# Sinkhorn attention and token mixer: X of two batches turned by SyncE transfers, step order searched anew

## The chip, the cores and the metric

The kernel runs on one core of one Trainium2 chip. A time is the device time of one execution in microseconds; the time before is the median of three runs, 105.33 us (105.27 to 105.39).

## The reference

Four batches of eight heads, 768 positions, 64 features per head. A sort matrix P of 8 by 8 per head mixes blocks of 96 positions of k and v, attention stays within a block, and its result x goes through a linear token mixer and an output product.

```python
P = sort_net
for _ in range(5):
    P = np.exp(P - np.max(P, axis=-1, keepdims=True))
    P = P / (np.sum(P, axis=-1, keepdims=True) + 1e-09)
    P = P / (np.sum(P, axis=-2, keepdims=True) + 1e-09)
k_sorted = np.einsum('bhij,bhjcd->bhicd', P, k_b)      # v alike
scores = scale * np.matmul(q_b, k_sb.transpose(0, 1, 2, 4, 3))
attn = np.exp(scores - max) / (sum + 1e-09)             # within a block
x = np.matmul(attn, v_sb)                               # then [batch, 768, 512]
wq, wk = x @ w_q, x @ w_k
W_tok = scale * np.einsum('bsd,btd->bst', wq, wk)
mixed = np.einsum('bst,btd->bsd', W_tok, x)
out = np.maximum(mixed, 0.0) @ w_out
```

## The kernel before, in words

The whole program is a list of steps in the string ORDER, one batch at a time being one digit. A loop at the end takes each word, say `T21:7`, and calls the function of its letter (`u_T`) with batch 2, part 1 and PSUM bank 7. Batches are counted from 0, so batch 2 is the third. Capital letters are matmuls on TensorE. Small letters are mostly the copies out of PSUM, with the engine behind the colon (A ScalarE, D VectorE, G GpSimd, S SyncE). Every engine and every DMA queue takes its steps in the order of the list; between engines, semaphores hold a step until its inputs are there and its PSUM bank or tile has been read. So the list fixes both what runs beside what, and what stands behind a step that waits.

The steps of one batch, in the order in which they depend on each other:

- `lq`, `lk`, `lv` (u_l, L220): GpSimd issues the loads of q, k, v of a batch from HBM, cast to bf16, 768 KB each as written. `lp` and `lo` load the weights. Qn, Kn and Vn have three buffers each.
- `Q`/`q`: q turned to QT on TensorE, copied out. Four parts, one per pair of heads. `K`/`k`: k sorted and turned to KT. `n` forms M, the sort matrix spread over masks, on GpSimd for batches 1 to 3.
- `V`/`v`: v sorted to Vs in three parts (batches 1 to 3). `R` (u_R, L313): six SyncE transfers per batch (1 to 3) that bring Vs into VT's layout, SBUF to SBUF, 132 KB each. Batch 0 takes `Y`/`y` and `F`/`f` on TensorE instead.
- `S`/`e`: scores and their exp into E, seven parts. `P`: E times VT into PSUM, five parts, with a column of row sums. `r` (reciprocal) and `x` (scaling, into X) on VectorE.
- `T`/`t` (u_T, L390; u_t, L394): X turned to XT, one part per pair of heads: eight transposing matmuls of 96x96 into one bank, then a copy.
- `J`/`j`: q and k projections from XT into qkT, in two halves, each needing all four parts of XT, one per matmul. `d`: half of qkT shifted by 64 partitions to qD, by SyncE or VectorE. `W`/`w`, `G`/`g`: the token mixer's inner product A from X. `H`/`h`: A times qkT and qD, with the relu, into mixT in three parts.
- `O`/`o`: output product, six per batch, into `ot` (four slots of 512 KB). `s` (u_s, L466): SyncE stores.
- `Z` is filler on TensorE while it has nothing to do, and `a`, `c`, `A`, `B`, `u`, `i` are the Sinkhorn loop and set-up at the start.

X and XT have two buffers each, as have QT, KT, VT and E. A function `u_D` (L386) that turns X by a transposing DMA, for two pairs of heads at once, is there; the ORDER of before doesn't use it. SyncE carries, in order: the sort matrix, six `R` for each of batches 1 to 3, two `d` for each of batches 0 to 2, and among these the stores. The last functions, a check of the softmax sums and a general path behind it, are not touched.

Of the kernel before, what the change touches and what calls it, by code (L numbers as in the profile page):

```python
# [14 lines left out]
NMIX = 2  # L15
SPQ = False
SPLIT = 6

ORDER = """
i02:D lq0 i00:G c00:D a01:A c01:D A00:0 a02:A:0 c02:D a03:A Z09:0 Q00:0 c03:D Q01:1 a04:A c04:D lk0  # L20
a05:A Q03:7 Q02:6 q01:A:1 c05:D Z06:2 B00:1 n00:D:1 n01:D:1 Z02:2 K00:2 K01:4 q00:A:0 k00:A:2
n02:D:1 u00:D:1 i03:G n03:D:1 K03:0 K02:2 k01:A:4 k02:D:2 k03:A:0 S00:4 S02:0 e00:A:4 q02:D:6 lv0
e02:A:0 Y02:2 q03:D:7 Y01:4 lv1 Y00:6 y01:D:4 Y03:0 y02:A:2 S04:2 y00:A:6 lk1 lq1 n10:G n11:G y03:D:0 S03:4
F01:6 F00:7 e04:A:2 S01:0 F03:2 e03:A:4 e01:A:0 f01:D:6 f00:D:7 V11:3 V12:5 f03:D:2 F02:7 P00:0
v11:A:3 v12:D:5 S05:2 f02:A:7 e05:A:2 r00:D:0 V10:4 n21:G P01:6 K13:2 x00:D:0 r01:D:6 P02:0
x01:D:6 v10:A:4 r02:D:0 K10:4 K12:6 k13:A:2 P03:2 x02:D:0 r03:D:2 k10:A:4 K11:4 k12:D:6 T01:0
T00:1 lp Q11:6 k11:A:4 t00:A:1 S06:4 U00:7 R12:S Q12:1 R15:S e06:A:4 R11:S x03:D:2 P04:2 t01:D:0
Q13:0 Q10:4 q11:A:6 r04:D:2 z01:A:7 S12:5 q12:D:1 x04:D:2 q13:A:0 U01:7 q10:D:4 z02:D:7 T02:1 T03:0
e12:A:5 t02:D:1 t03:D:0 lq2 S11:2 S10:4 S13:6 Q22:1 Q21:0 e11:A:2 q21:D:0 Q23:2 e10:A:4 q22:D:1
J00:3 e13:A:6 R10:S R14:S n20:G R13:S S16:4 e16:A:4 S15:0 j00:D:3 P11:6 S14:3 J01:5 e15:A:0 q23:D:2  # L30
e14:A:3 P12:0 r11:D:6 lk2 K23:2 j01:A:5 x11:D:6 K21:6 r12:D:0 P13:4 k23:A:2 K20:2 x12:D:0 k21:A:6
r13:D:4 n30:G K22:0 Q20:6 x13:D:4 W00:7 k20:A:2 lv2 k22:A:0 P14:2 lq3 V20:4 V22:0 d00:S q20:D:6
r14:D:2 W01:7 x14:D:2 V21:2 T12:6 v22:D:0 t12:D:6 v20:A:4 P10:4 S25:0 v21:A:2 S26:2 T13:6 r10:D:4
w00:A:7 T11:7 x10:D:4 d01:S e26:A:2 S23:2 n31:G e25:A:0 Q30:4 G00:5 S21:0 t13:D:6 e23:A:2 t11:D:7
S24:6 lk3 e21:A:0 G01:5 Q31:3 lv3 e24:A:6 g00:D:5 Q33:2 q31:D:3 S22:0 T10:5 e22:A:0 S20:6 q33:D:2
t10:D:5 K32:2 R21:S K31:0 J11:5 k32:A:2 R20:S q30:D:4 R22:S H00:2 Q32:4 e20:A:6 k31:D:0 lo j11:D:5
h00:A:2 R23:S K30:0 R24:S H01:6 q32:D:4 K33:4 h01:A:6 R25:S k30:D:0 P21:2 J10:0 V31:6 k33:A:4 P23:4
j10:A:0 v31:A:6 r21:D:2 P22:0 d10:S x21:D:2 r23:D:4 V32:2 W10:6 v32:A:2 W11:6 O01:7 x23:D:4 w10:A:6
V30:4 r22:D:0 v30:A:4 x22:D:0 o01:D:7 O02:2 S34:0 o02:D:2 H02:6 e34:A:0 h02:D:6 S32:3 O03:5 e32:A:3
o03:A:5 P20:0 T21:7 P24:2 r20:D:0 T22:4 t21:A:7 G10:5 G11:5 x20:D:0 r24:D:2 d11:S g10:D:5 S36:6  # L40
R32:S t22:A:4 S30:0 e36:A:6 R35:S O00:4 x24:D:2 S31:5 e30:A:0 R30:S H11:2 H10:0 O05:7 o00:D:4 T20:4
h11:D:2 o05:D:7 e31:A:5 R34:S T23:5 h10:A:0 t20:A:4 t23:A:5 S35:2 e35:A:2 R31:S S33:0 H12:6 e33:A:0
s01:S O04:4 J20:5 O10:3 s00:S j20:A:5 R33:S P31:0 J21:5 o10:A:3 P32:2 h12:D:6 O15:6 r31:D:0 o04:D:4
j21:A:5 r32:D:2 o15:A:6 x31:D:0 P33:4 r33:D:4 O12:7 o12:A:7 P30:0 x33:D:4 s02:S O13:6 d20:S P34:4
W20:7 x32:D:2 W21:7 r34:D:4 d21:S o13:A:6 T31:2 w20:D:7 O14:3 t31:D:2 r30:D:0 O11:7 G20:2 x30:D:0
G21:2 o11:A:7 s10:S x34:D:4 T30:7 o14:A:3 g20:A:2 t30:A:7 T32:0 T33:1 t32:D:0 t33:D:1 H21:4 H20:2
H22:6 h20:D:2 s11:S J30:0 J31:1 h22:D:6 O20:2 j30:D:0 O21:3 h21:A:4 W30:0 O22:7 j31:A:1 d31:D
w30:A:0 W31:0 o22:D:7 w31:D:0 O24:1 o20:A:2 o21:A:3 o24:A:1 G30:7 G31:7 g30:D:7 O23:0 d30:D H30:4
h30:A:4 o23:D:0 H31:2 s12:S h31:D:2 O25:7 s20:S H32:0 s21:S O31:4 o25:A:7 h32:D:0 O30:7 o31:D:4
s22:S s31:S O34:1 o34:A:1 o30:D:7 O32:4 O35:0 o32:A:4 s30:S o35:A:0 s34:S s32:S s35:S O33:4 o33:A:4  # L50
s33:S
"""


# [1 line left out]
def kernel(  # L56
# [12 lines left out]
    B, H, S, D = q.shape  # L69
    NB = sort_net.shape[-1]  # L70
    BLK = S // NB
# [29 lines left out]
    def tiles(name, n, shape, dtype=BF16):  # L101
        return [sb.tile(shape, dtype, name=f"{name}{i}") for i in range(n)]

    PS = psp.tile([P, 8, 512], FP32, name="ps")
    ENG = {"A": nc.scalar, "D": nc.vector, "G": nc.gpsimd, "S": nc.sync}
# [13 lines left out]
    X = tiles("X", 2, [BLK, NP, NB, P])  # L119
    XT = tiles("XT", 2, [P, PT, S])  # L120
# [7 lines left out]
    if SPQ:  # L128

        q32 = XT[0].rearrange("p t s -> p (t s)").bitcast(FP32).rearrange("p (h r d) -> p h r d", r=R6, d=D)  # L130
        nc.sync.dma_start(out=q32.rearrange("p h r d -> p h (r d)"),
                          in_=q[0, 0:H // 2].rearrange("h (p r) d -> p h (r d)", p=P))
# [251 lines left out]


    def u_D(b, n, e, bank):  # L386
        ENG[e].dma_start(out=XT[b % 2][:, 2 * n:2 * n + 2, :].rearrange("p k (i c) -> p (k i) c", c=BLK),
                         in_=X[b % 2][:, 2 * n:2 * n + 2].rearrange("c k i m -> c (k i m)"), transpose=True)

    def u_T(b, n, bank):  # L390
        for i in range(NB):
# [56 lines left out]
    def osplit(b, n):  # L448

        r, m = n % 10, n // 10  # L450
        return (r, slice(m * DM // 2, (m + 1) * DM // 2)) if b == B - 1 and r >= SPLIT else (r, slice(0, DM))

# [6 lines left out]
    def oslot(b, n):  # L459
        return ot[(b * 3 + n // 2) % NOT]  # L460
# [4 lines left out]

    def u_s(b, n, e, bank):  # L466
        od = out[b].rearrange("(p r) e -> p r e", r=R6)
        if b < B - 1:
            ENG[e].dma_start(out=od[:, 2 * n:2 * n + 2, :], in_=oslot(b, 2 * n))
        else:  # L470
            r, c = osplit(b, n)
            ENG[e].dma_start(out=od[:, r, c], in_=oslot(b, r)[:, r % 2, c])
# [172 lines left out]
    for item in ORDER.split():  # L645
# [5 lines left out]
        b, n = int(name[1]), int(name[2:])  # L651
# [41 lines left out]
```

## Time and profile before

| what | value |
|---|---|
| median of three runs | 105.33 us |
| the profiled execution: its time, its span | 105.29 us, 103.5 us |
| TensorE matmuls | 86.7 us, 84% of the span |
| VectorE | 71.8 us, 69% |
| ScalarE | 69.2 us, 67% |
| GpSimd | 25.4 us, 25% |
| chain of waits: TensorE, DMA, GpSimd | 44%, 39%, 6% |
| HBM read, written | 20.19 MB, 6.29 MB |
| granted TensorE clock | 0.998 |

The busy shares of three engines lie close together and are means over two different stages, so they don't say what bounds; the slices and the chain of waits do. [...] A DMA's row on SyncE is the time in which SyncE issues it, and its landing is told apart from that. Times in a timeline or chain are from the start of the span.

### The profile page before, as it was taken

The page shows a single profiled execution, that of the slowest core. Times are in us where ns is not written, and L with a number is a line of the kernel's source. Part 1 is how long each engine was busy: PE and PEld are TensorE (multiplying, and loading weights), DVE is VectorE, ACT ScalarE, POOL GpSimd, SP SyncE. Part 2 cuts the span into 40 slices and gives each one's busy share as a digit, 9 for nine tenths or more (in the row PEclk, how much of TensorE's full clock was granted, in tenths as well). Part 3 has the DMA queues.
Part 4 walks back from the last instruction along what each step waited for, and adds up shares of the span by engine and source line. Part 5 has one row for each costly group of instructions (what it writes and reads, how often), then busy time and mean ns, then how long its engine had stood idle before and what let it go on. Part 6 is the DMA issues. An engine that isn't in the chain of part 4 may idle for free.

```text
span 103.5 us, 3508 instructions
## 1 busy us (share of the span) xinstructions
PE 86.7 (84%) x1485; PEld 60.3 (58%) x1493; DVE 71.8 (69%) x142; ACT 69.2 (67%) x98; POOL 25.4 (25%) x42
## 2 busy tenths in 40 slices
PE   0297977996959699999969899999999999999930
PEld 0135366895838577898745675856667575543410
DVE  2676667889956578989559498777389979368400
ACT  4222479998668868979849688989944282633440
POOL 5992054991199500000000000000000272000000
PEclk9999999999999999999999999999999999999999
DMA  0899999999999999999999933737042077047782
GB/s 3 88 199 204 204 204 205 203 206 203 237 232 244 206 202 204 209 210 206 241 247 228 208 77 100 224 142 255 6 176 65 6 301 307 24 185 301 299 321 99
DMA packets 18593, 19.35 MB, mean 187 GB/s; under 512 B 912, under 2 KB 16656, under 8 KB 18576
## 3 DMA queue, kind: packets, MB, share of 16 engines
q0 software_dynamic: 13296, 10.09, 63.6%
q1 hardware_dynamic: 5280, 9.03, 25.2%
q8 instruction: 11, 0.18, 0.7%
q14 instruction: 6, 0.05, 0.1%
HBM read 20.19 MB, written 6.29 MB: 256 GB/s over the span
## 4 chain that ended last, share of the span: by engine, by line
PE 44%; DMA 39%; POOL 6%; ACT 3%; SPq 2%; issue 2%; POOLq 0%; ACTq 0%
PE ps L156 44%; DMA Kn<-in_k_dram 18%; DMA Vn<-in_v_dram 14%; DMA VT<-Vs 7%; SPq L314 2%; POOL Vn L231 2%; POOL M L252 1%; POOL Qn L231 1%; ACT Vs L160 1%; POOL Kn L231 1%; ACT KT L160 1%; ACT ot L160 1%; POOL E L211 1%; ACT wk L160 0%; POOL VT L217 0%
## 5 line engine op out<-in xcount | busy, mean ns | idle before, releaser
L352 ACT ACTIVATE E<-ps 96x960 bf16<-96x960 f32 (+1 forms) x28 | 23.9, 905 | 2.9 <-PE ps L156 2.9
L156 PE MATMUL ps<-wo,mixT 128*128 128x512 bf16 x89 | 22.8, 380 | 0.5 <-issue 0.2
L381 DVE TENSOR_TENSOR X<-ps,Rall 96x896 bf16<-96x896 f32 (+1 forms) x20 | 19.9, 1001 | 0.5
L160 ACT COPY ot<-ps 128x512 f32<-128x512 f32 (+1 forms) x16 | 9.2, 587 | 8.6 <-PE ps L156 8.0
L160 ACT CAST KT<-ps 128x768 bf16<-128x768 f32 x14 | 10.6, 806 | 4.9 <-PE ps L156 4.9
L156 PEld LDWEIGHTS <-mixT 128*128 128x128 bf16 x96 | 8.3, 98 | 9.1 <-issue 1.0
L484 POOL CROSS_LANE_REDUCE s<-Rall 96x1 f32<-96x280 f32 x1 | 0.8, 756 | 46.5 <-DVE Rall L376 46.5
L156 PE MATMUL ps<-VT,E 96*128 96x65 bf16 x256 | 11.4, 193 | 0.8 <-DMA VT<-Vs 0.7
L156 PEld LDWEIGHTS <-E 96*128 96x128 bf16 x256 | 9.9, 97 | 3.1 <-issue 0.8
L252 POOL TENSOR_TENSOR M<-PTR,m_p 128x512 bf16<-128x512 bf16 x6 | 7.8, 1314 | 11.6 <-PE ps L156 6.0
L156 PEld LDWEIGHTS <-KT 64*128 64x128 bf16 (+1 forms) x288 | 8.3, 97 | 3.5 <-issue 2.2
L156 PE MATMUL ps<-QT,KT 64*128 64x96 bf16 x256 | 9.2, 204 | 0.4 <-ACT KT L160 0.3
L156 PE MATMUL ps<-idb,Qn 128*64 128x128 bf16 x192 | 7.1, 221 | 2.6 <-DMA Qn<-in_q_dram 2.6
L446 DVE TENSOR_SCALAR mixT<-ps 128x1024 bf16<-128x1024 f32 x7 | 8.5, 1220 | 1.2 <-PE ps L156 0.7
L156 PE MATMUL ps<-M,Kn 128*64 128x128 bf16 x192 | 7.2, 221 | 2.4 <-DMA Kn<-in_k_dram 1.8
L376 DVE RECIPROCAL Rall<-ps 96x14 f32<-96x14 f32 (+1 forms) x20 | 4.6, 231 | 6.7 <-PE ps L156 5.5
L156 PEld LDWEIGHTS <-Qn 128*64 128x64 bf16 x192 | 5.9, 110 | 4.0 <-DMA Qn<-in_q_dram 3.3
L156 PEld LDWEIGHTS <-Kn 128*64 128x64 bf16 x192 | 6.0, 109 | 3.7 <-DMA Kn<-in_k_dram 2.6
L160 ACT CAST Vs<-ps 128x1024 bf16<-128x1024 f32 x7 | 7.1, 1014 | 1.4 <-PE ps L156 1.2
L162 DVE COPY QT<-ps 128x768 bf16<-128x768 bf16 x12 | 6.3, 545 | 2.0 <-PE ps L156 2.0
L162 DVE CAST KT<-ps 128x768 bf16<-128x768 f32 x6 | 5.6, 942 | 2.8 <-PE ps L156 2.8
L162 DVE COPY ot<-ps 128x512 f32<-128x512 f32 x9 | 6.0, 678 | 2.1 <-PE ps L156 2.1
(81 smaller groups left out, 132.1 us busy)
## 6 DMA issues: line engine op xcount, KB each, us to landing
out_dram<-ot SPq DMA_DIRECT2D x9, 512.0 KB, 2.9
Qn<-in_q_dram POOLq DMA_DIRECT2D x4, 768.0 KB, 16.3
Kn<-in_k_dram POOLq DMA_DIRECT2D x4, 768.0 KB, 17.6
Vn<-in_v_dram POOLq DMA_DIRECT2D x4, 768.0 KB, 14.8
VT<-Vs SPq DMA_DIRECT2D x18, 132.0 KB, 6.2
out_dram<-ot SPq DMA_DIRECT2D x6, 256.0 KB, 2.0
wo<-in_moe_w_out_dram POOLq DMA_DIRECT2D x1, 512.0 KB, 26.7
qD<-qkT SPq DMA_DIRECT2D x6, 48.0 KB, 2.3
```

The source lines that it names most:

```text
L156: nc.tensor.matmul(o, w, x, is_transpose=t, start=start, stop=stop, skip_group_check=True)
L160: nc.scalar.copy(o, i)
L162: nc.vector.tensor_copy(o, i)
L211: nc.gpsimd.memset(t[:, :, 2 * TH * BLK:EW], 0.0)
L231: nc.gpsimd.dma_start(out=t[b % NIN][:, h0:h1].rearrange("p h r d -> p h (r d)"), in_=src[b, h0:h1].rearrange("h (p r) d -> p h (r d)", p=P))
L252: ENG[e].tensor_tensor(out=M[b % 2][:, h0:h0 + hn], in0=src.unsqueeze(2).to_broadcast([P, hn, SP, NB]), in1=m_p.unsqueeze(1).unsqueeze(3). ...
L314: ENG[e].dma_start(out=VT[b % 2].rearrange("(s r) i h x -> r s i (h x)", r=R6)[n], in_=Vs[0][:, n].rearrange("p h e -> p (h e)"))
L352: nc.scalar.activation(E[b % 2][:, n, 0:2 * w * BLK].rearrange("p (t a c) -> p a t c", a=2, c=BLK), PS[0:BLK, bank:bank + 2, 0:w * BLK].re ...
L376: nc.vector.reciprocal(Rall[:, b, n, :, 0:w], avps(bank, w)[:, :, :, D])
L381: nc.vector.tensor_mul(xo.rearrange("p (a t d) -> p a t d", a=2, d=D), avps(bank, w)[:, :, :, 0:D], Rall[:, b, n, :, 0:w].unsqueeze(3).to_ ...
L446: nc.vector.tensor_relu(o, i)
L484: g.tensor_reduce(s1[:, 1:2], rv, axis=AX.XYZWC, op=ALU.max)
```

## The change

`u_D` now turns one pair of heads (XK = 1) instead of two, and takes the place of `T` and `t` in batches 2 and 3: eight steps `T20` to `T33` with their eight copies go, and eight transposing SyncE transfers `D20` to `D33` come. Batches 0 and 1 keep `T`. The rest of ORDER holds the same work, but its order, its PSUM banks and the engines of some copies are another result of the same search. The loads begin lq0 lv0 lk0 lp lq1 lk1 lv1 instead of lq0 lk0 lv0 lv1 lk1 lq1 lp; the other seven follow in the same order. The filler is 19 matmuls instead of 17. `u_s` has a way to split stores, which with ROWS empty issues the same ones.

The functions, and of ORDER (cut) the lines with the steps that matter here:

```diff
+XK = 1
+ROWS = ()
...
-i02:D lq0 i00:G c00:D a01:A c01:D A00:0 a02:A:0 c02:D a03:A Z09:0 Q00:0 c03:D Q01:1 a04:A c04:D lk0
...
-n02:D:1 u00:D:1 i03:G n03:D:1 K03:0 K02:2 k01:A:4 k02:D:2 k03:A:0 S00:4 S02:0 e00:A:4 q02:D:6 lv0
-e02:A:0 Y02:2 q03:D:7 Y01:4 lv1 Y00:6 y01:D:4 Y03:0 y02:A:2 S04:2 y00:A:6 lk1 lq1 n10:G n11:G y03:D:0 S03:4
...
-h00:A:2 R23:S K30:0 R24:S H01:6 q32:D:4 K33:4 h01:A:6 R25:S k30:D:0 P21:2 J10:0 V31:6 k33:A:4 P23:4
-j10:A:0 v31:A:6 r21:D:2 P22:0 d10:S x21:D:2 r23:D:4 V32:2 W10:6 v32:A:2 W11:6 O01:7 x23:D:4 w10:A:6
-V30:4 r22:D:0 v30:A:4 x22:D:0 o01:D:7 O02:2 S34:0 o02:D:2 H02:6 e34:A:0 h02:D:6 S32:3 O03:5 e32:A:3
-o03:A:5 P20:0 T21:7 P24:2 r20:D:0 T22:4 t21:A:7 G10:5 G11:5 x20:D:0 r24:D:2 d11:S g10:D:5 S36:6
-R32:S t22:A:4 S30:0 e36:A:6 R35:S O00:4 x24:D:2 S31:5 e30:A:0 R30:S H11:2 H10:0 O05:7 o00:D:4 T20:4
-h11:D:2 o05:D:7 e31:A:5 R34:S T23:5 h10:A:0 t20:A:4 t23:A:5 S35:2 e35:A:2 R31:S S33:0 H12:6 e33:A:0
...
-W20:7 x32:D:2 W21:7 r34:D:4 d21:S o13:A:6 T31:2 w20:D:7 O14:3 t31:D:2 r30:D:0 O11:7 G20:2 x30:D:0
-G21:2 o11:A:7 s10:S x34:D:4 T30:7 o14:A:3 g20:A:2 t30:A:7 T32:0 T33:1 t32:D:0 t33:D:1 H21:4 H20:2
-H22:6 h20:D:2 s11:S J30:0 J31:1 h22:D:6 O20:2 j30:D:0 O21:3 h21:A:4 W30:0 O22:7 j31:A:1 d31:D
...
+i02:D lq0 i00:G c00:D a01:A c01:D A00:3 a02:A:3 c02:D Z09:3 Q01:1 a03:A c03:D a04:A q01:A:1 c04:D
+lv0 Q03:3 a05:A c05:D Z010:0 B00:6 lk0 n03:D:6 Q00:1 i03:G n00:D:6 Y03:4 n02:D:6 q00:A:1 y03:D:4
+Y00:0 Q02:5 y00:A:0 q03:D:3 u00:D:6 n01:D:6 Y02:3 Y01:1 y02:A:3 q02:A:5 lp F03:0 lq1 K03:3 K00:6
+f03:D:0 y01:A:1 k03:D:3 K01:0 K02:3 F00:2 k01:A:0 k00:D:6 k02:D:3 S06:6 lk1 S05:0 lv1 n10:G e06:A:6
...
+k32:A:6 K33:6 e32:A:2 S24:2 e23:A:0 k33:D:6 e24:A:2 P20:4 V30:0 r20:D:4 x20:D:4 V31:6 V32:2 v30:A:0
+S31:4 e31:A:4 v31:D:6 R30:S G10:0 G11:0 v32:D:2 g10:D:0 R35:S S35:6 S33:4 O05:1 P23:2 r23:D:2
+e33:A:4 e35:A:6 d11:S R31:S O02:0 P22:6 d10:S O04:4 x23:D:2 r22:D:6 o05:A:1 x22:D:6 P21:2 R32:S
+R33:S o04:A:4 O00:1 r21:D:2 o00:A:1 s02:S x21:D:2 R34:S P24:6 O03:5 D21:S r24:D:6 x24:D:6 S34:3
+D20:S S30:1 H10:6 o03:D:5 o02:A:0 h10:D:6 D23:S e34:A:3 O01:0 e30:A:1 D22:S s01:S o01:A:0 P33:4
+H11:6 r33:D:4 S36:1 O10:3 e36:A:1 x33:D:4 P34:1 h11:A:6 o10:A:3 P32:4 r34:D:1 P31:6 J20:0 x34:D:1
+P30:2 D33:S J21:1 r31:D:6 j20:D:0 O11:0 s00:S j21:A:1 W20:1 r30:D:2 W21:1 x31:D:6 O13:6 x30:D:2
+d21:S r32:D:4 H12:2 w20:A:1 x32:D:4 G20:7 d20:S G21:7 g20:D:7 D30:S o11:A:0 O12:0 h12:A:2 D32:S
+o13:A:6 o12:A:0 H21:1 H20:4 D31:S H22:6 h20:D:4 O15:3 O14:0 s11:S O21:4 o15:A:3 h21:D:1 J30:3 J31:1
...
     def u_D(b, n, e, bank):
-        ENG[e].dma_start(out=XT[b % 2][:, 2 * n:2 * n + 2, :].rearrange("p k (i c) -> p (k i) c", c=BLK),
-                         in_=X[b % 2][:, 2 * n:2 * n + 2].rearrange("c k i m -> c (k i m)"), transpose=True)
+        t = slice(XK * n, XK * n + XK)
+        ENG[e].dma_start(out=XT[b % 2][:, t, :].rearrange("p k (i c) -> p (k i) c", c=BLK),
+                         in_=X[b % 2][:, t].rearrange("c k i m -> c (k i m)"), transpose=True)
...
     def u_s(b, n, e, bank):
         od = out[b].rearrange("(p r) e -> p r e", r=R6)
-        if b < B - 1:
-            ENG[e].dma_start(out=od[:, 2 * n:2 * n + 2, :], in_=oslot(b, 2 * n))
+        if b < B - 1 or n >= 20:
+            m = 2 * (n % 20)
+            w = 1 if b in ROWS else 2
+            for r in range(0, 2, w):
+                ENG[e].dma_start(out=od[:, m + r:m + r + w, :], in_=oslot(b, m)[:, r:r + w, :])
```

More of the change, by code (lines that the diff above doesn't have):

```diff
@@ L17 @@
 SPLIT = 6
+XK = 1
+ROWS = ()
 ORDER = """
-i02:D lq0 i00:G c00:D a01:A c01:D A00:0 a02:A:0 c02:D a03:A Z09:0 Q00:0 c03:D Q01:1 a04:A c04:D lk0
-a05:A Q03:7 Q02:6 q01:A:1 c05:D Z06:2 B00:1 n00:D:1 n01:D:1 Z02:2 K00:2 K01:4 q00:A:0 k00:A:2
-n02:D:1 u00:D:1 i03:G n03:D:1 K03:0 K02:2 k01:A:4 k02:D:2 k03:A:0 S00:4 S02:0 e00:A:4 q02:D:6 lv0
-e02:A:0 Y02:2 q03:D:7 Y01:4 lv1 Y00:6 y01:D:4 Y03:0 y02:A:2 S04:2 y00:A:6 lk1 lq1 n10:G n11:G y03:D:0 S03:4
-F01:6 F00:7 e04:A:2 S01:0 F03:2 e03:A:4 e01:A:0 f01:D:6 f00:D:7 V11:3 V12:5 f03:D:2 F02:7 P00:0
@@ L25 @@
[L25 to L36, printed above, removed]
@@ L42 @@
-h11:D:2 o05:D:7 e31:A:5 R34:S T23:5 h10:A:0 t20:A:4 t23:A:5 S35:2 e35:A:2 R31:S S33:0 H12:6 e33:A:0
-s01:S O04:4 J20:5 O10:3 s00:S j20:A:5 R33:S P31:0 J21:5 o10:A:3 P32:2 h12:D:6 O15:6 r31:D:0 o04:D:4
-j21:A:5 r32:D:2 o15:A:6 x31:D:0 P33:4 r33:D:4 O12:7 o12:A:7 P30:0 x33:D:4 s02:S O13:6 d20:S P34:4
-W20:7 x32:D:2 W21:7 r34:D:4 d21:S o13:A:6 T31:2 w20:D:7 O14:3 t31:D:2 r30:D:0 O11:7 G20:2 x30:D:0
-G21:2 o11:A:7 s10:S x34:D:4 T30:7 o14:A:3 g20:A:2 t30:A:7 T32:0 T33:1 t32:D:0 t33:D:1 H21:4 H20:2
-H22:6 h20:D:2 s11:S J30:0 J31:1 h22:D:6 O20:2 j30:D:0 O21:3 h21:A:4 W30:0 O22:7 j31:A:1 d31:D
@@ L48 @@
[L48 to L51, printed above, removed]
+i02:D lq0 i00:G c00:D a01:A c01:D A00:3 a02:A:3 c02:D Z09:3 Q01:1 a03:A c03:D a04:A q01:A:1 c04:D
+lv0 Q03:3 a05:A c05:D Z010:0 B00:6 lk0 n03:D:6 Q00:1 i03:G n00:D:6 Y03:4 n02:D:6 q00:A:1 y03:D:4
@@ new lines @@
+Y00:0 Q02:5 y00:A:0 q03:D:3 u00:D:6 n01:D:6 Y02:3 Y01:1 y02:A:3 q02:A:5 lp F03:0 lq1 K03:3 K00:6
+f03:D:0 y01:A:1 k03:D:3 K01:0 K02:3 F00:2 k01:A:0 k00:D:6 k02:D:3 S06:6 lk1 S05:0 lv1 n10:G e06:A:6
+F02:5 S01:6 F01:3 f00:D:2 e05:A:0 e01:A:6 f02:D:5 S03:0 S04:4 e03:A:0 f01:D:3 Q10:2 Q11:3 U00:6
+e04:A:4 q11:D:3 P04:0 n11:G Q12:3 r04:D:0 z01:A:6 P03:4 q12:A:3 q10:D:2 S02:6 e02:A:6 K11:2 x04:D:0
+r03:D:4 x03:D:4 K10:0 K13:6 P02:4 k11:D:2 k10:A:0 Q13:3 S00:0 lq2 q13:D:3 k13:A:6 r02:D:4 x02:D:4
+e00:A:0 P01:6 r01:D:6 S10:2 V10:0 V11:4 n21:G e10:A:2 v11:A:4 x01:D:6 n20:G P00:2 v10:D:0 V12:6
@@ new lines @@
+r00:D:2 R12:S v12:A:6 lk2 K12:4 k12:D:4 T03:0 S12:6 t03:A:0 U01:1 x00:D:2 T01:0 R10:S t01:D:0
+z02:D:1 S13:2 e12:A:6 T02:0 S16:6 R14:S e13:A:2 e16:A:6 S11:3 S14:1 t02:D:0 n31:G T00:5 S15:6
+t00:D:5 R11:S Q22:5 Q20:0 q20:D:0 e11:A:3 e15:A:6 R13:S K21:3 lv2 K20:6 q22:D:5 e14:A:1 Q23:5
+k21:A:3 k20:D:6 R15:S Q21:2 q23:A:5 P12:0 q21:A:2 S20:3 P13:6 J00:5 e20:A:3 S22:2 r12:D:0 x12:D:0
+r13:D:6 P11:0 J01:4 e22:A:2 x13:D:6 V22:2 r11:D:0 T12:7 j00:A:5 x11:D:0 lq3 j01:A:4 v22:A:2 d00:S
+t12:D:7 P10:4 S21:0 r10:D:4 T11:6 d01:S n30:G W00:7 x10:D:4 V21:2 e21:A:0 t11:D:6 R24:S W01:7
@@ new lines @@
+v21:A:2 P14:0 V20:4 T10:6 K23:2 r14:D:0 w00:A:7 Q32:7 R25:S x14:D:0 k23:A:2 Q33:0 v20:D:4 Q30:1 lk3
+q33:D:0 G00:5 q30:A:1 K22:2 k22:A:2 R23:S q32:D:7 t10:D:6 G01:5 S25:0 g00:D:5 T13:7 lv3 t13:D:7
+e25:A:0 R22:S R20:S H02:4 h02:A:4 H01:2 J11:6 h01:D:2 lo J10:0 S26:4 j10:D:0 R21:S e26:A:4 K31:1
+Q31:3 K30:4 j11:D:6 k31:A:1 k30:A:4 W10:0 W11:0 q31:D:3 K32:6 S32:2 H00:4 w10:D:0 S23:0 h00:D:4
+k32:A:6 K33:6 e32:A:2 S24:2 e23:A:0 k33:D:6 e24:A:2 P20:4 V30:0 r20:D:4 x20:D:4 V31:6 V32:2 v30:A:0
+S31:4 e31:A:4 v31:D:6 R30:S G10:0 G11:0 v32:D:2 g10:D:0 R35:S S35:6 S33:4 O05:1 P23:2 r23:D:2
@@ L52 @@
+o13:A:6 o12:A:0 H21:1 H20:4 D31:S H22:6 h20:D:4 O15:3 O14:0 s11:S O21:4 o15:A:3 h21:D:1 J30:3 J31:1
+s10:S j30:D:3 j31:D:1 d30:D o14:A:0 O22:5 O20:1 o22:D:5 h22:A:6 W30:0 o21:A:4 w30:A:0 W31:7 O23:5
+w31:A:7 o20:A:1 G30:0 s12:S o23:D:5 G31:0 g30:D:0 O24:1 d31:D H31:4 s21:S H32:6 O25:0 H30:2 s20:S
+h31:D:4 h32:A:6 O32:4 o24:D:1 O33:1 h30:D:2 o25:A:0 o32:A:4 o33:A:1 O35:5 o35:A:5 s22:S s32:S O30:4
+o30:A:4 O31:0 O34:7 o31:A:0 o34:A:7 s33:S s35:S s30:S s31:S s34:S
 """
```

## Prediction

> **What bounds the kernel now.** I read the page's slices first, then the chain of waits in order of time, then TensorE's timeline. In the slices PE is TensorE's busy tenths and DMA those of the 16 DMA engines; a slice is 2.59 us.
>
> ```profile
> PE   0297977996959699999969899999999999999930
> DMA  0899999999999999999999933737042077047782
> ```
>
> The DMA engines are full for 22 slices, to about 57 us: the loads of q, k and v. Behind that they are mostly idle and TensorE is full. The chain says the same, with the place where it changes over:
>
> ```profile
> 29.34 14.51 DMA Vn<-in_v_dram
> ...
> 49.73 7.52 DMA VT<-Vs
> 57.26 0.14 issue
> 57.39 0.22 PE ps L156 x2
> ...
> 92.78 6.56 PE ps L156 x31
> ```
>
> Columns: start, length, what. It hangs on loads to 43.84 us (v of the third batch), then on its sorted v going through SyncE (landed 57.26), and from 57.39 us on nothing but TensorE, to 99.34. The fourth batch's v is issued at 33.35 us and takes the tile's longest landing, 25.0 us: it lands at 58.4. So a saving counts where TensorE does less after 57.4 us, and only if no wait opens there.
>
> What the change takes out stands in that stretch, as TensorE's timeline shows:
>
> ```profile
> 65.27 0.50 PE L156 MATMUL ps<-idb,X 96*128 96x96 bf16 x8
> 65.61 0.41 PE L156 MATMUL ps<-VT,E 96*128 96x65 bf16 x8
> 65.86 0.50 PE L156 MATMUL ps<-idb,X 96*128 96x96 bf16 x8
> 66.29 1.06 PE L156 MATMUL ps<-X,wk 96*64 96x256 bf16 x16
> ...
> 70.29 0.84 PE L156 MATMUL ps<-idb,X 96*128 96x96 bf16 x16
> 71.07 0.30 PE L156 MATMUL ps<-QT,KT 64*128 64x96 bf16 x6
> ```
>
> "idb,X" is a T step. Lengths overlap, so a step's price is the distance to the next start: 0.34, 0.43, and 0.78 for two. T31 (79.81 to 80.16) and the last three (82.97 to 84.10) give 0.35 and 1.13. **Eight T steps are 3.03 us of TensorE.**
>
> **The change, part by part.** Removed: those 3.03 us and eight copies XT<-ps (0.55 us each on VectorE, 0.81 on ScalarE), which lay beside TensorE and gain nothing by themselves.
>
> Moved, after the order in which each engine's instructions now stand: ahead of the third batch's first P step go J10 (0.65), W10 and W11 (0.51), one S step (0.20) and one H step (0.22), 1.58 us. So from that P to the last O, TensorE needs 57.39 to 99.33 = 41.94, less 3.03, less 1.58, about **37.3 us**.
>
> When does that P start? I laid the written order end to end, each step starting when its engine is free and its inputs are there, with row prices: spacings as above for TensorE (O 0.87, P 0.44, J 0.65, T 0.35, K and Q 0.33), E 0.91, VT issues 0.59. For the order of before this puts J30 at 84.9 us, where the trace has 84.86. The first v now comes second, and the second batch's v seventh. Six loads had landed by 29.54 and the two small weights by 30.84, so that v is there at about 30.2, not 20.8. Its VT transfers go out at 32.5 to 35.7 us; under load they take 6.2 to 7.2, so its P12 starts at 42, where P11 stood at 38.2. TensorE idles some 2 us more between 30 and 42. The third batch's last V step then runs at 48.7 rather than 44.96, its last VT transfer is issued at 52.0 rather than 49.7 and lands 6.3 to 7.5 later, 58.3 to 59.5. **P20 starts at 59.2, 1.8 later.** The fourth batch's v (58.4) is there by then, so V30 to V32 wait for nothing. The price of the reorder is 1.8; 57.39 + 1.8 + 37.3 = 96.5 against 99.33 is -2.8; laid end to end, with the new small waits, -2.5. I use -2.5.
>
> Two more filler matmuls (17 to 19, near 10 us) and v before k at the start lie under the wait for the second load (12.8 us): nothing. If that cover failed, two fillers are 0.43. GpSimd's loads now stand behind a mask product that waits for the second batch's V: lv2 leaves at 34 us, with lk2 landing at 39.7; the queue doesn't run dry. The output loop issues the same stores.
>
> **Added: eight transposing transfers** of 96x1024 bf16 (192 KB, 256 B runs) on SyncE. The trace has none. The nearest rows are the VT transfers, SBUF to SBUF on the same queue:
>
> ```profile
> L314 SPq DMA_DIRECT2D VT<-Vs x18: 546/588/1490, 22.6 to 69.9; - x18
> ...
> DMA to landing us min/median/max: 2.3/6.2/7.5
> ```
>
> The first line is the time that SyncE is held by one issue, in ns (median 588); the second the landing. Lower end: 0.59 us of SyncE each and 2.35 us to land. Upper end: SyncE held in proportion to the runs, 768 of 256 B against 128 in a VT transfer, 6 x 0.59 = 3.5 us. Linear between qD (64 runs, 0.50) and VT (128, 0.59) it would be 1.5. I take **1.2 us**, nearer to the VT row, which shares queue and memories.
>
> Third batch: SyncE must first issue the six R3 transfers, the two qD and s02, so D21 leaves at 68.8 us. J20 is reached by TensorE at 74.06 and needs D22, the fourth, at its third matmul, 0.33 later. Four of 1.2 us: 68.8 + 3 x 1.2 + 2.35 = 74.75: **a wait of 0.4**. While it waits, P30, J21 and all O steps of the second batch stand behind it on TensorE, and on VectorE j20 stands ahead of r30, x31, x30, x32, so the fourth batch slips by the same. Fourth batch: D33, s00, the two d, D30, D32, D31. x32 is done about 5.1 us after J20 starts, J30 comes 9.1 after; D31 leaves one issue behind D32 and lands 2.35 later: 5.1 + 1.2 + 2.35 = 8.65, no wait. Sum: -2.5 + 0.4 = -2.1. The profiled run was 105.29 (span 103.5 and 1.79 around it; median of the runs 105.33): 103.2. If a transfer landed in the 2.9 of an output store, J20 would wait 0.5 more (-1.6); with most of the weight on the VT row I take -2.0, **103.3**.
>
> By the ends: SyncE 0.59 gives -2.5, 102.8. Each 0.1 us above 1.1 costs 0.3 at J20; above 1.5 J30 waits too, 0.24 per 0.1. At 1.75, -2.5 + 2.0 + 0.5 = 0, the break-even. At 2.05 it is +2.0 (2.97, 1.17 and 0.35 of outputs queued behind); at 3.5, J20 7.3 and J30 4.3, and SyncE itself is the bound: about +14, 119.
>
> [...]
>
> **Rivals.**
> 1. *SyncE is held over 1.75 us by each transfer* (the other side). Place: D21 to D22 ahead of J20, D30 to D31 ahead of J30; price as above, 106 to 119. For it: the 256 B runs, six times as many as in VT, and nothing else ready for TensorE to take meanwhile, its order being fixed. Against it: store rows hold SyncE 0.33 us for 512 KB, so the size alone is no price. 0.27. [...]
> 2. *Slow landing, cheap issue.* Stores of 512 KB run in the same stretch, and VT transfers beside them landed in 4.3 to 4.6 us at 64 to 65 us. With 4 us and 0.85 to 1.15 of SyncE, J20 waits 1.0 to 1.9 and J30 0.9 to 1.2: -0.6 to +0.6, 104.7 to 105.9. 0.14.
> 3. *The late second batch costs more than 1.8.* The third batch's VT and the fourth's k and v cross at 52 to 59 us; if P20 started at 61.5, all of the gain but 0.2 were gone: 105.1, and slower with any wait at J20. 0.07.
>
> **How the numbers follow.** Forecast (issue 0.6 to 1.5 us, waits under 1.3): 102.6 to 104.4, chance 0.52. 0.2% of the time, 0.21 us, is about what a measurement here can tell from none. Faster: 0.52 and 0.04 of rival 2, 0.56. Same: 0.06, from rival 2. Slower: 0.27, 0.04 and 0.07, 0.38. Range 102.3 to 108.5: below the forecast's own range only a few hundredths are left, and above 108.5 (issue over 2.2 us) 0.15. The forecast's own range is 102.6 to 104.4.
>
> **What would show it.** TensorE's timeline: first P of the third batch near 59.2, J20 near 74.5, J30 near 83.5, last O near 96.6. SyncE's rows: the transposing issues near 1.2 us, landings under 3. Right if waits for XT stand under 1 us in sum; wrong if TensorE waits for XT several us twice, or if the P starts past 60.

## The result, and the profile after

The changed kernel takes 110.12 us (median of four runs, 109.14 to 110.76) where the kernel before took 105.30 beside it: 1.045 times as long, with a 95% interval of 1.037 to 1.054. Ratios, here and below, are taken over the executions of each kernel that lie within 1.5% of its fastest one. The forecast was 103.3, with a range up to 108.5. The profiled execution took 110.5 us, span 108.7, against 105.29 and 103.5 before.

The slices of the page (a slice is now 2.72 us; PEclk is the granted clock of TensorE in tenths, 9 for full):

```profile
PE   0299978997898863999799899995839999999960
...
PEclk9999999999999999599999999999985999999998
```

Before, PE had no hole behind its 22nd slice, and PEclk was 9 throughout. Now there are two holes (slices 15 and 16, and 28 to 30), and right behind each the clock falls to half (slices 17 and 31). The chain of waits in order of time (start, length, what) shows what ends them:

```profile
8.59 20.82 DMA Vn<-in_v_dram
...
35.01 7.26 DMA VT<-Vs
...
42.40 11.16 PE ps L157 x222
...
71.57 3.23 DMA VT<-Vs
...
76.36 4.24 DMA XT<-X
80.63 24.40 PE ps L157 x172
```

The second batch's v holds up its VT transfers, and these hold up P12 at 42.40. In the fourth batch TensorE waits for the last VT transfer (issued at 71.57), and J20 for D22 (issued at 76.36, landed 4.24 us later). TensorE's timeline gives the lengths in brackets, with the step that waited:

```profile
42.40 0.60 PE L157 MATMUL ps<-VT,E 96*128 96x65 bf16 x14 [2.12 <-DMA VT<-Vs]
...
74.94 0.59 PE L157 MATMUL ps<-VT,E 96*128 96x65 bf16 x14 [1.19 <-DMA VT<-Vs]
...
80.63 0.80 PE L157 MATMUL ps<-XT,wqk 128*128 128x384 bf16 x2 [2.22 <-DMA XT<-X]
...
82.01 1.47 PE L157 MATMUL ps<-XT,wqk 128*128 128x384 bf16 x4
```

The last line is J21: 1.47 us from its first matmul's start to its last one's end, where each J of the third batch took 0.81 before. That is the half clock. The table by stretch (stretch, length, PE busy with its instructions, then the other engines, PEclk, DMA share, GB/s), first the two stretches ahead of and behind the third batch's first P, then each window at half clock, then the window of the same length ahead of each:

```profile
0.00:62.10 62.10, 50.03 (x1014) 38.09 (x1015) 45.48 (x99) 42.38 (x58) 22.21 (x35) 0.97 1.17 193
62.10:105.10 43.00, 39.45 (x418) 22.33 (x418) 26.53 (x40) 23.09 (x37) 3.23 (x7) 0.96 0.62 193
43.03:46.45 3.42, 3.42 (x46) 2.16 (x45) 2.57 (x4) 1.25 (x2) 0.00 (x0) 0.50 1.31 201
80.58:83.99 3.41, 3.36 (x22) 1.93 (x22) 2.24 (x4) 0.43 (x1) 0.00 (x0) 0.50 0.84 191
39.62:43.03 3.41, 1.29 (x44) 1.11 (x39) 0.96 (x1) 1.96 (x3) 0.00 (x0) 1.00 1.30 222
77.17:80.58 3.41, 1.24 (x30) 0.95 (x29) 1.13 (x3) 0.69 (x2) 0.00 (x0) 1.00 0.80 237
```

Both windows are 3.41 us long, and TensorE was idle for 2.12 and 2.17 us of the 3.41 us just ahead. At the granted 0.50, a matmul stream that fills such a window does half its work in it: about 1.7 us lost each time, an estimate from clock and length.

SyncE's own timeline and the row of the transposing transfers (ns of SyncE: least, median, most; first and last start) with their landing in us:

```profile
71.57 0.55 SPq L315 DMA_DIRECT2D VT<-Vs  x1
72.22 5.42 SPq L389 DMA_TRANSPOSE XT<-X  x4
```

```profile
L389 SPq DMA_TRANSPOSE XT<-X x8: 1229/1278/2357, 72.2 to 87.9; - x8
...
DMA to landing us min/median/max: 2.6/2.9/4.2
```

An issue holds SyncE for 1.28 us (median), more than twice the 0.59 of a VT transfer. D23, D30, D32 and D31, beside a store for at most the end of their way, land in 2.6 to 2.7 us; D20 and D21, which began while the store s02 was in flight, took 3.14 and 3.66. The two that took over 4 us, D22 and D33, had one thing more beside them: a packet of 16 KB on the queue that the page calls instruction, from 78.45 to 79.40 us. The view of the DMA queues from 78.4 to 79.5 us has it (packets, MB, share):

```profile
q8 instruction: 1, 0.02, 5.4%
```

### The profile page after: what moved, and what is told of

Same layout as the page of the kernel before. It is cut to its first block, busy times and chain, and to the rows that moved or that the text cites. A ratio compares the mean times of both kernels' runs of the same rounds, so it can differ in the third digit from the quotient of the medians.

```text
span 108.7 us, 3365 instructions
## 1 busy us (share of the span) xinstructions
PE 89.5 (82%) x1431; PEld 60.4 (56%) x1431; DVE 72.0 (66%) x138; ACT 66.0 (61%) x94; POOL 25.4 (23%) x42
## 4 chain that ended last, share of the span: by engine, by line
PE 47%; DMA 33%; POOL 7%; DVE 4%; issue 2%; ACT 2%; SPq 2%; POOLq 0%; DVEq 0%
PE ps L157 47%; DMA Vn<-in_v_dram 19%; DMA VT<-Vs 10%; DMA XT<-X 4%; POOL Qn L232 2%; POOL Kn L232 2%; SPq L315 1%; DVE Vs L163 1%; ACT ot L161 1%; DVE X L382 1%; POOL ot L224 1%; DVE KT L163 1%; DVE mixT L448 1%; POOL Vn L232 1%; ACT XT L161 1%
## 5 line engine op out<-in xcount | busy, mean ns | idle before, releaser
L157 PE MATMUL ps<-wo,mixT 128*128 128x512 bf16 x96 | 23.8, 384 | 0.0
L161 ACT COPY ot<-ps 128x512 f32<-128x512 f32 (+1 forms) x21 | 12.2, 587 | 5.9 <-PE ps L157 5.9
L157 PEld LDWEIGHTS <-E 96*128 96x128 bf16 x256 | 10.5, 102 | 6.2 <-issue 2.6
L161 ACT CAST KT<-ps 128x768 bf16<-128x768 f32 x12 | 9.4, 802 | 3.6 <-PE ps L157 3.5
L157 PEld LDWEIGHTS <-KT 64*128 64x128 bf16 (+1 forms) x288 | 9.0, 99 | 4.3 <-issue 2.5
L157 PE MATMUL ps<-QT,KT 64*128 64x96 bf16 x256 | 9.9, 209 | 0.9 <-ACT E L353 0.5
L157 PE MATMUL ps<-XT,wqk 128*128 128x384 bf16 x32 | 8.0, 386 | 2.2 <-DMA XT<-X 2.2
L161 ACT COPY QT<-ps 128x768 bf16<-128x768 bf16 x7 | 5.6, 810 | 3.9 <-PE ps L157 3.9
L163 DVE CAST KT<-ps 128x768 bf16<-128x768 f32 x8 | 7.5, 951 | 0.4 <-PE ps L157 0.4
L157 PE MATMUL ps<-fil 128*128 128x512 bf16 x19 | 6.2, 492 | 1.8 <-ACT m_p L175 1.8
```

The lines of the kernel that those rows point to most:

```text
L157: nc.tensor.matmul(o, w, x, is_transpose=t, start=start, stop=stop, skip_group_check=True)
L161: nc.scalar.copy(o, i)
L163: nc.vector.tensor_copy(o, i)
```

## The experiments

Four questions: what the transfers cost and what the order costs, what the half clock costs, what SyncE's 1.28 us depends on, and whether the transfers pay anywhere. All ratios are to the kernel before in the same runs (105.4 us).

### First four: transfers, order, half clock

**e1** keeps the new order and puts the eight T and their copies back; **e2** only the four of the third batch.

The edit of e2, in ORDER's words; in e1 also D30 to D33, in the same manner:

```diff
+T22:4
...
+t22:A:4
...
-D21:S
...
-D20:S
...
+T23:5
...
-D23:S
+t23:A:5
...
+T21:3
+t21:D:3
...
-D22:S
...
+T20:0
...
+t20:D:0
```

> The new order with the eight transposing transfers taken out again and eight T steps with their copies put in (banks 0, 1, 3, 4, 5, 7; all work done). Theory A, the loss is made of four pieces: the third batch's first P is 2.9 us later than forecast because TensorE idled 2.1 us for the second batch's VT and then ran a 3.4 us window at half clock; 1.2 us waiting for the fourth batch's VT; 2.2 us waiting for XT at J20; a second half-clock window behind that wait, about 1.7. Then this removes 2.2 + 1.7 and adds eight T steps, 3.0: near 109.2, still slower than before by 3 to 4. Rival B, the transposing transfers are the whole loss: 105 to 106. Rival C, the order alone is the whole loss: 110 or more.

> The new order with T steps in the third batch only; the fourth batch keeps its four transposing transfers, for which the changed kernel showed no wait (J30 at 91.45, D31 landed at 90.61). Theory A: minus 2.2 and 1.7, plus four T steps, 1.5: about 107.7. If the fourth batch's transfers cost something that the trace doesn't show as a wait (SyncE held, stores later), it comes out no better than the kernel with all turns back, 109.

Measured: e1 108.1 us, ratio 1.023 (1.020 to 1.026); e2 108.17, 1.020 (1.012 to 1.029). So the new order without one transfer already costs 2.3% (2.4 us), and the transfers 2 us on top, of which nothing is left when the third batch's are taken out. e1 came out 1.1 us under its theory A (109.2), which had left the wait of 1.19 us for VT in the sum; e1 and e2 have no such wait. e2 was expected 1.5 us under e1 and is as fast as it: the four T taken out of its fourth batch gave nothing that the runs can tell. In the traces its last O ends 0.7 us earlier than e1's (101.87 against 102.60), after a new wait of 0.51 us for a copy of outputs, and the span behind it is 0.6 us longer. In e1's profile the third batch's first P starts at 62.20, as in the changed kernel, with one window at half clock (43.94 to 47.35) behind the wait of 2.05 us ahead of P12. Behind that P, TensorE works 40.3 us with T steps of 2.85 us among them (by distance to the next start): 37.5 without, near the forecast's 37.3. Three of those T stand ahead of P33, the first P of the fourth batch, which TensorE reaches without waiting:

```profile
74.82 0.60 PE L158 MATMUL ps<-VT,E 96*128 96x65 bf16 x14
```

That is 12.62 us behind e1's first P of the third batch. In the changed kernel, without these T, P33 comes 12.86 us behind it, since its VT transfer lands no sooner. So 1.0 us of T taken out there became a wait.

**e3** is the changed kernel with eight filler matmuls (fil, no use) ahead of P12 and eight ahead of J20, where TensorE would wait in any case.

```diff
+Z08:0
 P12:0
...
+Z08:0
 J20:0
```

> The changed kernel with eight filler matmuls of 128x512 ahead of the first P of the second batch and eight ahead of J20, into a free bank: 1.7 us each, less than the waits of 2.1 and 2.2 us that stand there. Theory A with the half clock as a piece of its own: both windows stay at full clock, 1.5 to 1.7 us each saved, 106.7 to 107.5, and a granted clock of 0.99. Rival, the waits alone make the loss and the clock only follows: 110 as the changed kernel, or more.

Measured: ratio 1.024 (1.018 to 1.030), so 107.9 us, 0.4 above the range expected and 2.2 less than the changed kernel, though TensorE has sixteen matmuls, some 3.5 us, more to do. The granted clock in e3's slices:

```profile
PEclk9999999999999999999999999999999999999999
```

No half clock is left in the profiled execution; two others had a mean clock of 1.000 as well, and the fourth, at 112.5 us, one of 0.982. P12 starts at 42.47, as in the changed kernel (42.40), but the third batch's first P at 60.13 instead of 62.08. The half clock is a cost of its own, and both its windows come from the idle time ahead of them. It does not account for all: 2.5 us over the kernel before remain.

**e4** is the order of before, each T replaced by its D in place, the copies dropped.

```diff
-T21:7
+D21:S
...
-t21:A:7
```

> The order of before, its eight T steps and copies replaced where they stand by the eight transposing transfers (issued at the places of the T steps). Issue 1.26 us and landing 2.65 to 4.2 as in the changed kernel: the last x of the fourth batch stands just ahead of J30 there, so J30 waits about 3.8 us for XT and H2 about 1 us, TensorE saves 3.0, and a half-clock window behind the wait adds up to 1.7: 108.7 to 110.5. Rival C, the transfers are harmless and the order is the loss: 105 or less.

Measured: 116.8 us, ratio 1.106 (1.102 to 1.110): far beyond what was expected. The slices and the first waits of TensorE (engine, line, waited for: us in all, times, longest):

```profile
PEclk9999999999999999999999999975599975599997
```

```profile
PE ps L157 <- DMA XT<-X: 5.1, 4, 2.1
PE ps L157 <- DMA out_dram<-ot: 3.1, 1, 3.1
```

The expectation had priced waits for XT and one half clock. There are four windows of it, and a wait of 3.15 us that it did not have: the fourth batch's first P at 78.53 waits for VT transfers that stand behind the D's on SyncE (the last leaves at 74.44 and lands at 78.33; before, it left at 69.94). The row names a store as the last to land, but the P reads VT. A transfer put where a T stood thus delays what SyncE has to issue next, too.

### SyncE's time: per transfer or per size

**e8** is the changed kernel with one transfer for two pairs, four in all.

```diff
-XK = 1
+XK = 2
...
-D21:S
...
-D23:S
...
-D22:S
+D21:S
...
-D33:S
...
-D32:S
```

> The changed kernel with one transposing transfer for two head pairs, two per batch (96 x 2048) instead of four. If SyncE is held per transfer: 1.3 us each, D21 is issued some 2.6 us earlier than the last one before, J20 waits less than 1 us, and there is one window at half clock instead of two: 107 to 108.5. If it is held by size: 2.5 us each, landings as late as before, J20 waits about 2 us: 109.5 to 111.

Measured: 107.32 us, ratio 1.020 (1.016 to 1.024). The row of its transfers:

```profile
L389 SPq DMA_TRANSPOSE XT<-X x4: 1421/1554/1763, 71.0 to 83.0; - x4
...
DMA to landing us min/median/max: 3.5/3.9/4.2
```

Twice the size holds SyncE for 1.55 us instead of 1.28, so most of the time is a price per transfer. The four of the third batch took SyncE from 72.22 to 77.64, two take it from 71.01 to 74.52. J20 (from 76.69) no longer waits. So merging them wins back 2.8 of the 4.8 us.

Its profiled execution also had no half clock up to the last O, though TensorE waited 2.12 us ahead of P12 as before; its other executions, 0.2 to 1 us longer, had a lower mean clock (0.977 to 0.982 against 0.991). The trace shows why the wait cost nothing here. In all fourteen traces, every change of the granted clock lies a whole number of 3.413 us behind the first one recorded; the two half-clock windows of the changed kernel start 37.55 us apart, 11 times that. In e8 the clock changes 7.59 us into the span and again at 103.17, 28 windows later, so that a border between two windows lies at 41.73. It cuts the wait (40.25 to 42.37) in two:

```profile
38.31:41.73 3.42, 1.72 (x48) 1.45 (x48) 1.98 (x3) 2.94 (x4) 0.92 (x2) 1.00 1.26 231
41.73:45.14 3.41, 2.77 (x65) 2.14 (x66) 2.00 (x4) 1.27 (x2) 0.00 (x0) 1.00 1.31 204
```

TensorE idles 1.7 us in the one window and 0.6 in the other. e8 serves below as the changed kernel without half clock.

### The load order

**e12** loads the second batch's v ahead of its k, and puts its V steps ahead of S02 and K11.

```diff
-S06:6 lk1 S05:0 lv1
+S06:6 lv1 lk1 S05:0
...
-q12:A:3 q10:D:2 S02:6 e02:A:6 K11:2
+q12:A:3 q10:D:2 V10:2 V11:6 v11:A:6 v10:D:2 V12:2 v12:A:2 S02:6 e02:A:6 K11:2
```

> The changed kernel with the second batch's v loaded ahead of its k, and its V steps ahead of S02 and K11 with other banks; all else in the changed kernel's order. Theory A (the wait ahead of P12 comes from v being the seventh load, and the first half clock from that wait): last VT transfer of the second batch lands 3 to 4 us earlier, near 39, no wait ahead of P12 and no window at half clock near 43; but k now comes later, so the 2.1 us of waiting return in smaller pieces at K11 and behind it, and the third batch's first P starts at 60 to 61 instead of 62.1, as in the run with fillers (60.1). Wait for XT and second window stay: 107.8 to 109. Rival (the late loads cost nothing but that wait): first P of the third batch at 58 to 59, 106 to 107. Rival (the wait is not the cause of the half clock): a window at half clock near 43 all the same, 109.5 to 111.

Measured: 109.12 us, ratio 1.034 (1.029 to 1.039), just above theory A's range. The VT transfers land by 38.73 instead of 42.27, and the wait ahead of P12 is gone. But TensorE's timeline shows where it went:

```profile
25.73 1.05 PE L157 MATMUL ps<-Vn,M 128*128 128x128 bf16 x16 [1.12 <-DMA Vn<-in_v_dram]
...
29.57 1.25 PE L157 MATMUL ps<-M,Kn 128*64 128x128 bf16 x36 [0.92 <-DMA Kn<-in_k_dram]
...
34.05 0.59 PE L157 MATMUL ps<-VT,E 96*128 96x65 bf16 x14 [1.06 <-ACT E L353]
```

The waits return in smaller pieces, P12's batch starts no earlier (43.06) and the third batch's first P comes at 61.44, with full clock in this execution, 0.86 later than in e8. So theory A held in kind and not in size (the P was expected at 60 to 61); the rival that the wait at P12 was all the delay fell. Up to that P TensorE works 48.22 us and idles 13.22 in e12, 48.26 and 12.32 in e8, 45.22 and 12.17 in the kernel before: what makes the P late is more work ahead of it and the loads that feed it in this order, not one wait.

### The old head with a new tail

The rest keeps the order of before up to the load of w_out (or, in e5 to e7, nearly to P20) and has another order behind it. **e5** has all eight transfers, **e6** four (fourth batch), **e7** none.

> The order of the kernel before up to the first P20 (loads, banks and all), and behind it an order of its own, with all eight transposing transfers and no T. Theory A (most of the loss lies in the first half of the new order: the wait ahead of P12, the half clock behind it and the work put ahead of the third batch; the transfers save their TensorE time where SyncE is not crowded): third batch's first P at 57.4 as before; from there 41.4 us of TensorE work less 2.8 us of T, with 0.5 to 2.5 us of idle time, so the last O ends at 96.5 to 98.5 and the kernel takes 102.5 to 104.5. Theory B (the transfers bring a wait for XT of 2 us or more and a half clock behind it in any order): 105 to 108, with a window at half clock behind 73.

> The same head, the T of the third batch on TensorE, transposing transfers in the fourth batch alone. Theory A: 1.4 us of T come back, and no wait for XT at J20; 103.5 to 105. Theory B: J30 waits for its transfers, 105 to 106.5.

> The same head, all eight T on TensorE, behind P20 an order of its own. It tells what the transfers give from what the order behind P20 gives. Theory A: 104.3 to 105.5, so 1 to 2 us above the one with eight transfers. Rival: the order behind P20 is the gain and the transfers none; then this one is as fast as that with eight.

These three compute something else in one place: r34 in e5, r20 and r24 in e6, r20 in e7 names another bank than its P writes, so those reciprocals are of other numbers. The kernel ends with a check of the reciprocals on GpSimd, which then sent it into a general computation of 75 ms. Their times tell nothing; the profile up to there does, since the steps ahead are the same work. The last O ends at 99.12 in e5, 101.56 in e6 and 102.06 in e7, against 99.33 before. So, by one execution and one order each, the kernel with eight transfers is 2.9 us ahead of the one with none where the head is the old one, but e5 is only 0.2 us ahead of the kernel before: the new tail gave the rest away, and e5 missed the 96.5 to 98.5 expected. Two things cost it. V30 waits 0.7 us for its bank. And TensorE's timeline of e5 (first fence), beside that of before (second), shows a price that e5's forecast lacks:

```profile
61.99 1.03 PE L157 MATMUL ps<-wo,mixT 128*128 128x512 bf16 x4
62.95 0.39 PE L157 MATMUL ps<-QT,KT 64*128 64x96 bf16 x10
63.27 1.04 PE L157 MATMUL ps<-wo,mixT 128*128 128x512 bf16 x4
```

```profile
63.96 1.04 PE L156 MATMUL ps<-wo,mixT 128*128 128x512 bf16 x4
64.83 0.60 PE L156 MATMUL ps<-VT,E 96*128 96x65 bf16 x14
```

From an O (128 rows of the array, "128*128") to an S (64 rows, "64*128") it is 0.96 us; from an O to a P, 0.87. From S to O it is 0.32; from S or H to another of them, 0.21 or 0.22. The steps with 64 columns (K, Q, G) show it too: in the trace of before, a K or Q starts 0.12 us behind a P's last matmul, an O or T 0.03; a G starts 0.31 us behind an O's last, a P or T 0.22. So a change between S or H, the steps with 64 columns and the others costs about 0.1 us here. Behind the third batch's first P the written order of before has 19 such changes, e5 has 32: 1.3 us by this price.

**e9**, **e10** and **e11** mend both: each r reads its own bank, and S and H stand together (23, 18 and 17 changes). e9 has eight transfers, e10 four of two pairs each, e11 none. The core of e10:

```diff
-XK = 1
+XK = 2
...
+g10:D:0 r20:D:1 R35:S x20:D:1 P24:6 R31:S o05:A:3 R34:S S33:0 S30:2 o00:D:5 e33:A:0 H10:4 D20:S
+r24:D:6 h10:A:4 x24:D:6 H11:6 h11:D:6 O04:0 P33:4 e30:A:2 r33:D:4 P31:6 S36:2 O10:1 x33:D:4 e36:A:2
+D21:S s01:S r31:D:6 P34:2 s00:S o10:A:1 r34:D:2 x34:D:2 x31:D:6 o04:A:0 s02:S J20:4 J21:1 P30:2
...
+G20:7 d20:S G21:7 o11:A:0 d21:S O12:2 o13:A:6 g20:A:7 H21:3 h21:A:3 H22:0 H20:6 h20:D:6 O14:5 O15:3
+D31:S O21:6 D30:S h22:D:0 J30:7 o12:A:2 s10:S o14:A:5 s11:S j30:A:7 o21:A:6 J31:2 O20:5 o15:A:3
```

> The order of the kernel before up to its load of w_out, all eight transposing transfers, and from there an order searched anew: S and H steps stand together (in the last runs a TensorE step behind O began 0.96 us after it when it was S or H, 0.86 when it was P or T, so every change of kind costs 0.1 us), and each reciprocal reads the bank of its own P. Theory A (the transfers give what the T cost where SyncE is free for them): first P of the third batch near 57.5, last O at 96.5 to 98, 102.3 to 103.8. Theory B (transfers bring waits and a half clock in any order): 105 or more, with a window at half clock behind 73.

> As the one with eight transfers, but one transfer for two head pairs, so four in all, and an order of its own behind the load of w_out. Each holds SyncE 1.4 to 1.8 us (as in the run with two pairs) instead of 2.6 for two. If SyncE's time still matters it is 0.3 to 1 us faster than with eight: 102 to 103.3. If not, it is the same within 0.3 us.

> The same head, all T on TensorE as before, behind the load of w_out an order searched in the same way. It tells the order's worth from the transfers'. Theory A: 104.2 to 105.2, 1.5 to 2.5 us above the one with eight transfers (T takes 2.8 us of TensorE). Rival (the order is all): as fast as the one with eight, within 0.5 us.

| kernel | us | ratio (95%) | first P of third batch | last O ends |
|---|---|---|---|---|
| e9, eight transfers | 104.4 by the ratio, median of six 107.3 | 0.991 (0.988 to 0.994) | 57.25 | 101.92, with a half clock |
| e10, four of two pairs | 103.94 | 0.987 (0.984 to 0.989) | 57.45 | 97.48 |
| e11, none | 106.39 | 1.011 (1.009 to 1.013) | 57.35 | 99.77 |

All three missed what was expected of them: e10 by 0.6 us and e11 by 1.2, and e9's profiled execution shows theory B's wait and half clock. With the old head the transfers win: e10 is 2.4 us faster than e11, which has an order searched in the same way, and 1.4 us faster than the kernel before. Each stands for one order only, and e11 is itself 1.0 us slower than the kernel before, so how much of e10's lead is the transfers and how much the order is not shown beyond that. e10 is the fastest of all kernels here. Its D20 to J20 distance is 5.1 us (68.92 to 74.05), the first batch's stores are issued behind both transfers of the third, and TensorE shows no wait for XT; from its first P of the third batch to the last O it idles 0.4 us:

```profile
57.45:97.50 40.05, 39.65 (x444) 22.91 (x444) 24.90 (x37) 26.64 (x42) 3.23 (x7) 1.00 0.70 216
```

e9's six executions took 104.1, 104.6, 106.5 and three times 108.1 us, the profiled one among the last; its ratio has the first two. The profiled one shows what costs:

```profile
77.31 0.33 PE L157 MATMUL ps<-XT,wqk 128*128 128x384 bf16 x1 [2.41 <-DMA XT<-X]
```

J20 waits 2.41 us for a transfer of one pair that landed in 4.98, and a window at half clock starts at 77.49. e10's five executions (103.6 to 104.2 us) show no such spread.

## Why the prediction was wrong

The forecast's own sum ran from the third batch's first P: 59.2, 37.3 us of TensorE, a wait of 0.4. In the trace it is 62.08, 39.45 us of work and 3.49 of idle time.

- **Bound, and eight T at 3.03 us: right as a price (2.85 in e1), wrong as a gain.** With the T gone TensorE reached waits for VT and XT instead: the three T ahead of P33 gave nothing, and the fourth of that batch stood ahead of J20, which then waited 2.22 us.
- **37.3 us from that P to the last O: right as full-clock work.** e1 less its T gives 37.5; e8 has 37.9. The changed kernel's 39.45 has one half-clock window in it. What was missing is that a wait can be paid twice, as idle time and as half clock behind it.
- **P12 at 42, 2 us more of idle time ahead of it: right** (42.40, a wait of 2.12 us). What that wait sets off, the half clock, was not in the sum.
- **"P20 starts at 59.2, 1.8 later": the first step that failed.** The third batch's first P came at 62.08, 4.7 later than the 57.39 of before. The stretches up to it, of the kernel before and of e8:

```profile
0.00:57.39 57.39, 45.22 (x984) 34.95 (x986) 41.88 (x96) 41.89 (x58) 22.22 (x35) 1.00 1.21 199
0.00:60.58 60.58, 48.26 (x1013) 37.26 (x1014) 45.17 (x99) 42.44 (x58) 22.20 (x35) 1.00 1.20 198
```

  The kernel before works 45.22 us and idles 12.17 up to there, e8 works 48.26 and idles 12.32, the changed kernel 50.0 and 12.1. So 3.0 us is more work ahead of that P, 0.15 more idle time, and 1.5 the first half clock. Of the work, 1.58 were counted as moved and 0.43, by the forecast's own price, are the two fillers that it put at nothing; the other 1.0 is not told apart here. The moved work was taken off the stretch behind P20 but not charged ahead of it: laid end to end it had fallen into idle time, and in the trace the idle time did not shrink. The transfers for P20 are late too: the last leaves at 53.86 instead of 52.0 and lands at 60.85, forecast up to 59.5, and TensorE reaches the P 1.2 later still. In e8, without half clock, both meet (landing 60.45, P 60.58). Rival 3 had this outcome (61.5, given 0.07), but its reason, transfers slowed where they cross with loads, explains little: they landed in 6.05 to 7.32 us, much as forecast (up to 8.3 in e8).
- **SyncE at 1.2 us each: right** (1.28). The rival that had carried most of the slower side (over 1.75) was wrong, and the kernel became slower by other ways. Beside a VT transfer of two thirds the size, the issue takes more than twice as long (1.28 us against 0.59) and an undisturbed landing little longer (2.65 against 2.3).
- **Landing in 2.35 us, "a wait of 0.4" at J20: wrong in size.** D22 landed in 4.24, beside a store that left SyncE 1.4 us behind it and beside the instruction packet. Counted from the third batch's first P, D21 left 0.5 us later than forecast, D22 another 0.5, its landing took 1.9 more: 3.0 in sum. J20 was reached 1.0 later itself, so it waited 2.22. This was rival 2's mechanism, at 0.14, though stores alone do not explain it: the two VT landings of 4.3 and 4.6 us before, on which rival 2 went, also had an instruction packet beside them (65.78 to 67.52).
- **"V30 to V32 wait for nothing": true, but the wait stood one step later.** R34, the last VT transfer of the fourth batch, leaves SyncE behind s02 at 71.57, and P33 waits 1.19 us for it. The forecast priced SyncE's queue for what it does to D21, not for what reads VT. e8 and e12 have this wait too (1.45, 1.4); e1 and e2, with T steps in that place, don't.
- **No wait at J30: right.** D31 landed at 90.61, J30 started at 91.45.
- **Half clock: missing in every step.** Two windows, some 3.4 us of lost work by their length, 2.2 by e3. Without them the kernel is still slower: e3 2.4%. How many windows a kernel gets also depends on where their borders fall (in e8 one fell into the wait, at 41.73); the spread of the changed kernel, from 109.14 us at a mean clock of 0.984 to 110.76 at 0.966, may come from that.

In numbers: 2.9 us too late at P20, 2.15 more work, 3.1 more idle time behind it make the 8.1 us between the forecast's last O (96.9 by its sum) and 105.02. The sign "last O near 96.6" does not fit the forecast's own -2.0 us, which puts it at 97.3; nothing hangs on that.

What stays open: how the new head's delay divides among single steps (e12 tried one move, and the P came no earlier than in e8), and whether J20 would have waited without the instruction packet.

## What to carry to other kernels

Price a wait on TensorE by what follows it as well: here, behind each stretch of 3.41 us with 2.05 to 2.51 us idle, the clock was at half, by estimate 1.7 us per window, and with filler work in two such waits it was not (e3). Whether such a wait falls into one window or across a border seems to change from run to run (mean clocks of e8's four executions: 0.991, 0.977 and twice 0.982). A transfer that replaces TensorE work needed its queue free more for the count of transfers than for their bytes (1.28 us for one pair, 1.55 for two), so merge them, and look for what else the queue must still issue behind them. A change of order that moves work ahead of a stage must be charged there; compare the busy and idle time up to the stage's first step, not the stage alone. And time taken off an engine counts only as far as the next thing that it waits for comes earlier, too.

## What the runs showed of the hardware that was not expected

- **A window of 3.413 us with 2.05 us idle was enough for a half clock behind it.** The clock changed on a grid of 3.413 us in all fourteen traces, as shown under e8. Laid on that grid, from the first full clock to the last O, all seven windows in which TensorE idled 2.05 to 2.51 us (two each in the changed kernel and e4, one each in e1, e2 and e9) were followed by one at half clock, in e4 by two; of the full-clock windows that idled up to 1.8 us none was. So e8's wait of 2.12 us and e12's of 2.28 brought none because each lies across a border (e8: 1.7 and 0.6 us idle in its two windows; e12: 1.5 and 0.8, border at 79.53).
- **A transposing transfer from SBUF to SBUF cost SyncE mostly by the piece:** 1.28 us for 96x1024, 1.55 (e8) and 1.42 (e10) for 96x2048 in bf16.
- **Landings were longer beside stores (3.14 and 3.66 us against 2.6 to 2.7), and longer still beside an instruction packet.** Of the 56 single-pair transfers in eight traces, the eleven that landed in 3.86 us or more (up to 4.98) all had a 16 KB packet of the instruction queue in flight; no other took over 3.66, stores or not. In e9, D22 of the third batch took 4.33 with no store at all; the queue's line from 63.9 to 68.2 us:

```profile
q8 instruction: 1, 0.02, 1.6%
```

  No run moved such a packet, so this is a coincidence in all traces, not a tested cause.
- **A change of TensorE's row or column mode cost about 0.1 us:** from an O, 0.96 us to an S (e5) against 0.87 to a P (before).
